# Ten segment banks in ten bursts in a row, and four rows of a unit by ScalarE's relu of a difference

## The chip, the cores and the metric

The kernel runs on one core of one Trainium2 chip. A core has five engines that run side by side: TensorE (matrix products), VectorE, ScalarE (activation functions), GpSimd and SyncE, which here only issues DMAs. TensorE writes to PSUM, eight banks of 128 partitions by 2 KB; VectorE and ScalarE read the banks. The metric is the device time of one execution in microseconds, the lower the better. In the profile PE is TensorE, PEld its weight loads, DVE is VectorE, ACT is ScalarE, POOL is GpSimd and SP is SyncE.

## The reference

Two attention layers over the same 2048 x 512 input are mixed by a sigmoid gate. Side A is full attention with 32 heads of 16 dimensions. Side B works in four segments of 512 rows: causal attention inside a segment, mixed with a linear memory of the earlier segments.

```python
def _A_ref(x, wqkv, wo):
    ...
    scores = jnp.einsum("bhqd,bhkd->bhqk", q, k) * scale
    p = _softmax(scores, axis=-1)
    o = jnp.einsum("bhqk,bhkd->bhqd", p, v)
    return (lambda x, *d: x.transpose(*d))(o, 0, 2, 1, 3).reshape(B, S, D) @ wo
...
    for s in range(N):
        qs, ks, vs = q[:, :, s], k[:, :, s], v[:, :, s]
        logits = jnp.einsum("bhqd,bhkd->bhqk", qs, ks) * scale + mask
        p = _softmax(logits, axis=-1)
        a_dot = jnp.einsum("bhqk,bhkd->bhqd", p, vs)
        ...
        o = g * a_mem + (1.0 - g) * a_dot
...
    a = _A_ref(x, A_wqkv, A_wo)
    b = _B_ref(x, B_wq, B_wk, B_wv, B_wo, B_beta)
    return g * a + (1 - g) * b
```

Every softmax needs the maximum of each row of scores. For side A a row has 2048 keys, in four chunks of 512.

## The kernel before

**Units and slots.** The work of both attentions is cut into units: four heads by 512 queries. A full-attention unit ("A", 32 of them) has 64 slots, a segment unit ("B", 32) has 10. They alternate A, B, A, B (line 102), so a pair has 74 slots, and all pairs have 2368. One slot of the main loop (line 1004) does two things with a bank of PSUM each:

- `score_part` (line 714): a product of 128 keys by 512 queries with the row maximum already subtracted (it stands in two extra rows of q), into one of three `st` banks; ScalarE takes the exp of it into `p` (line 752).
- `max_part` (line 214), for a slot 96 further on (`LEAD`): a product of 128 queries by 512 keys into one of four `sm` banks (`banks[m % 4]`), from which VectorE takes the maximum of each row. A unit needs all its maxima before its scores start; hence the lead.

The product of `score_part` uses one half of TensorE's rows and that of `max_part` the other, so the two of a slot run at once.

After each third slot (`BURST`) come value products (`some_values`, line 764; a handful of 128-query pieces, three or four as `most()` says, line 993), or three of the products of an output block or of a later q tile (`shared`, line 1017), and now and then the transpose of a unit's maxima (line 1027). What is issued between two such places is called a burst here: three score and three maximum products, and what follows them.

**Which bank is whose.** The list `maxs` (line 114) writes the order of the maximum products out by hand. A full-attention unit has 64 banks: four key chunks `kc`, four blocks `s` of 128 queries, four heads; one reduce over 512 columns each (line 226). A segment unit has ten banks with causal pieces: six with two pieces of 128 and 384 or of 256 and 256 columns, four with one piece of 512 (line 232). For these VectorE runs a fused add-and-minimum with a mask, and reads its accumulator out (line 238). The second piece of a bank is issued only after the next bank's reduce (`flush_rows`). A segment unit's banks stand among those of a full-attention unit, always at the first slot of a burst, at distances of 9 and 3 slots in turn (`apart`, line 119): two bursts with one, two without. In the first and last units they stand in each burst.

**Loads.** `load_q` and `load_k` (lines 147 and 157) bring a unit's q and a chunk of keys from DRAM by SyncE's queue, `PRE` = 20 slots ahead of their first maximum product. `NKA` = 8 and `NKB` = 2 buffers hold chunks of keys. A chunk goes in four DMAs: 32 and 16 rows for each half of TensorE's rows.

**Before the loop**, the first 310 us compute q, k and v of both sides (`qk_tile`, line 362, and `v_tiles`) and the memory, and the first 96 slots' maxima. Each q or k is split into two halves of the short fp32 type and stored in DRAM.

Of the kernel before, what the change touches and what calls it, by code (L numbers as in the profile page):

```python
# [19 lines left out]
D = 512  # L20
# [22 lines left out]
PRE = 20  # L43
NKA, NKB = 8, 2
# [3 lines left out]
def gated_mix(ctx, tc, x, xT, wqkv, a_wo, b_wq, b_wk, b_wv, b_wo, beta, gate_w, out):  # L48
# [96 lines left out]
    knext = {"A": 0, "B": 0}  # L145
# [11 lines left out]
    def load_k(u, kc):  # L157

        side, g, c = u
        t = kbuf[side][knext[side] % len(kbuf[side])]  # L160
        knext[side] += 1
        src = kd[side, g // 2, kc]
        for r in range(2):
            hs = slice(4 * (g % 2) + 2 * r, 4 * (g % 2) + 2 * r + 2)
            nc.sync.dma_start(raw(t)[64 * r:64 * r + 32], src[:, hs])
            nc.sync.dma_start(raw(t)[64 * r + 32:64 * r + 48], src[0:16, hs])
        kt_[u, kc] = t
# [46 lines left out]
    def max_part(m, bank):  # L214
# [3 lines left out]
        if u not in pmt:  # L218
            pmt[u] = mp.tile([128, 4, 4] + [4] * (side == "A"), F32, tag="pm" + side, name="pm")
        pm = pmt[u]  # L220
        ps = bank()
        if side == "A":

            kc, s, h = i // 8, i % 8 // 2, 2 * r + i % 2
            max_product(ps, u, h, s, 0, CH, kt_[u, kc])
            nc.vector.tensor_reduce(pm[:, h, s, kc:kc + 1], ps, axis=AX.X, op=ALU.max)  # L226
            flush_rows()
# [35 lines left out]
    def loads(m):  # L263

        m = min(m, len(maxs) - 1)
        while loaded[0] <= m:
            u, (r, i) = maxs[loaded[0]]
            if loaded[0] == first_max[u]:
                load_q(u)
            kc = u[2] if u[0] == "B" else i // 8  # L270
            if (u, kc) not in kt_:
                load_k(u, kc)
            loaded[0] += 1
# [3 lines left out]
    with ExitStack() as p0:  # L277
# [84 lines left out]
        def qk_tile(side, w, xc, o, dst, then=None):  # L362

            ps = pr_ps.tile([128, CH], F32, tag="pr", name="pr")
# [6 lines left out]
            def e0():  # L371
                nc.scalar.copy(full, ps)  # L372
                nc.scalar.copy(q1, full)  # L373
                nc.sync.dma_start(dst[0:16].rearrange("d h t -> (d h) t"), raw(q1))
                if then:
# [100 lines left out]
        for c in range(NCH):  # L476
# [8 lines left out]
            for o in range(NO):  # L485
                qk_tile("A", wAk, xc, o, kd["A", o, c])
# [206 lines left out]

    tri["rest"] = dp.tile([128, CH], F32, name="rest")
# [309 lines left out]
    while n < nS or queue or beside or filled[0] < len(fill):  # L1004
# [5 lines left out]
        if m < nS:  # L1010
            loads(m + PRE)

            max_part(m, lambda: banks[m % 4])
        run_todo(m)
# [67 lines left out]
```

## Time and profile before

| what | value |
|---|---|
| time, median of 3 runs | 1786.52 us (1785.98 to 1787.45) |
| span of the profiled execution, first to last instruction | 1784.1 us |
| mean granted TensorE clock | 0.999 |
| TensorE busy, main loop (330 to 1700 us) | 1369.95 of 1370 us |
| VectorE busy, same stretch | 1367.91 us |
| ScalarE busy, same stretch | 1211.58 us |
| GpSimd busy, same stretch | 544.55 us |

No time of the profiled execution is known beside its span; the median of the runs is 2.4 us above it. In the views below a row reads: start and duration in us, engine, line of the kernel, operation, tile written <- tiles read, shapes, count; in brackets the idle time of the engine ahead of it and what ended it. Rows with a count over 1 are several instructions merged, from the first start to the last end. Instructions of an engine overlap in their fill, so a row of seven is shorter than seven times one. "x" in a view by stretches counts instructions.

### The profile page before, as it was taken

To read this page: it belongs to the slowest core of one execution; us is meant where nothing else is said; L and a number is where in the kernel's file an instruction comes from. 1 tells how busy PE (TensorE), PEld (TensorE's weight loads), DVE (VectorE), ACT (ScalarE), POOL (GpSimd) and SP (SyncE) were. 2 spreads that over 40 slices of the span, in tenths; PEclk is the share of its full clock that TensorE was granted. 3 is DMA by queue.
4 is the path that set the end of the run, shared out by engine and by line. 5 is a ranking of instruction groups with operands and counts; after the bars stand their busy time and mean duration, and the time that the engine had idled before them with its cause. 6 is when DMAs were issued, how large, how long until landed. Compare 5 with 4: busy or idle time off the path is not lost.

```text
span 1784.1 us, 40690 instructions
## 1 busy us (share of the span) xinstructions
PE 1774.3 (99%) x14945; PEld 913.3 (51%) x14945; DVE 1574.0 (88%) x3330; ACT 1437.8 (81%) x2753; POOL 641.0 (36%) x748
## 2 busy tenths in 40 slices
PE   9999999999999999999999999999999999999999
PEld 7887776444444444444444444444444444444444
DVE  4235777999999999999999999999999999999931
ACT  5455444888888888888888888888888888888884
POOL 3002222414161416443434343343434253435343
PEclk9999999999999999999999999999999999999999
DMA  6667556435463446645454545454545354544542
GB/s 222 211 222 258 190 192 191 140 97 146 107 165 108 134 121 174 152 132 135 132 139 128 146 127 145 128 145 113 154 111 154 118 141 116 147 121 136 144 162 61
DMA packets 142278, 261.55 MB, mean 147 GB/s; under 512 B 36312, under 2 KB 60408, under 8 KB 141568
## 3 DMA queue, kind: packets, MB, share of 16 engines
q1 hardware_dynamic: 140864, 257.82, 49.9%
q8 instruction: 119, 1.95, 0.5%
q0 software_dynamic: 1216, 1.14, 0.3%
q14 instruction: 79, 0.65, 0.1%
HBM read 174.39 MB, written 83.25 MB: 144 GB/s over the span
## 4 chain that ended last, share of the span: by engine, by line
PE 94%; DVE 2%; DMA 1%; ACT 1%; POOL 1%; issue 0%; SPq 0%; POOLq 0%; DVEq 0%; ACTq 0%
PE ops L786 33%; PE st L729 27%; PE sm L205 14%; PE pr L311 10%; PE ops L898 4%; PE ops L669 2%; PE sm L898 2%; POOL mn L377 1%; DMA raw<-xT 1%; PE num L499 0%; DVE pm L226 0%; DMA qdB<-q 0%; ACT ex L384 0%; DVE q L380 0%; PE mt_ps L196 0%
## 5 line engine op out<-in xcount | busy, mean ns | idle before, releaser
L752 ACT ACTIVATE p<-st 128x512 f32<-128x512 f32 x2261 | 1189.2, 600 | 152.8 <-PE sm L205 100.7
L226 DVE TENSOR_REDUCE pm<-sm 128x1 f32<-128x512 f32 x2048 | 1281.0, 683 | 11.8 <-PE sm L205 11.6
L729 PE MATMUL st<-qA,kA 50*128 50x512 f32 x2014 | 663.1, 432 | 0.0
L205 PE MATMUL sm<-kA,qA 48*128 48x512 f32 x2048 | 658.7, 428 | 0.2
L786 PE MATMUL ops<-p,vA 128*17 128x128 f32 (+3 forms) x6432 | 552.0, 441 | 0.0
L729 PEld LDWEIGHTS st<-qA,kA 50*128 50x128 f32 x2014 | 327.4, 185 | 415.2 <-ACT p L752 371.0
L205 PEld LDWEIGHTS sm<-kA,qA 48*128 48x128 f32 x2048 | 330.4, 185 | 15.6 <-issue 7.1
L848 POOL TENSOR_TENSOR rcp<-rec,minus 128x32 f32<-128x32 f32 x43 | 234.2, 5447 | 75.7 <-DMA rec<-dend 71.0
L238 DVE CUSTOM_DVE_ANT_0 rest<-sm,mask 128x128 f32<-128x128 f32 (+3 forms) x512 | 247.3, 483 | 1.9 <-PE sm L205 0.5
L786 PEld LDWEIGHTS ops<-p,vA 128*17 128x17 f32 x6432 | 130.4, 96 | 215.1 <-issue 190.1
L733 POOL TENSOR_SCALAR_AFFINE_SELECT p<-p 128x512 f32<-128x512 f32 x128 | 79.5, 637 | 324.1 <-ACT p L752 319.6
L205 PE MATMUL sm<-kB,qB 48*128 48x128 f32 (+3 forms) x512 | 166.0, 384 | 0.0
L729 PE MATMUL st<-qB,kB 50*128 50x512 f32 (+1 forms) x495 | 109.1, 329 | 0.3 <-ACT mt L199 0.3
L380 DVE TENSOR_TENSOR q<-full,q 128x512 fp32r<-128x512 f32 x56 | 38.9, 694 | 74.4 <-ACT q L373 74.4
L729 PEld LDWEIGHTS st<-qB,kB 50*128 50x128 f32 x495 | 69.8, 186 | 59.3 <-ACT p L752 48.8
L786 PE MATMUL ops<-p,vB 128*17 128x128 f32 (+3 forms) x1504 | 87.5, 350 | 0.0
L187 POOL CAST ms<-nm 128x16 fp32r<-128x16 f32 x32 | 6.7, 209 | 203.9 <-DVE nm L183 202.0
L205 PEld LDWEIGHTS sm<-kB,qB 48*128 48x128 f32 x512 | 79.9, 184 | 0.0
L377 POOL TENSOR_SCALAR mn<-full 128x512 f32<-128x512 f32 x24 | 35.7, 1489 | 101.7 <-ACT full L372 81.3
L372 ACT COPY full<-pr 128x512 f32<-128x512 f32 x56 | 32.7, 584 | 42.7 <-PE pr L311 42.4
L187 POOL CAST ms<-pm 128x16 fp32r<-128x16 f32 x32 | 6.3, 197 | 128.2 <-DVE pm L238 128.1
L864 POOL TENSOR_TENSOR v<-v,inv 128x512 f32<-128x512 f32 x31 | 39.9, 1286 | 25.7 <-DMA inv<-rdA 21.7
(188 smaller groups left out, 1628.9 us busy)
## 6 DMA issues: line engine op xcount, KB each, us to landing
kA<-kdA SPq DMA_DIRECT2D x256, 128.0 KB
vA<-vdA SPq DMA_DIRECT2D x31, 544.0 KB
kA<-kdA SPq DMA_DIRECT2D x256, 64.0 KB
kdA<-q SPq DMA_DIRECT2D x32, 256.0 KB
qdB<-q SPq DMA_DIRECT2D x32, 256.0 KB
qA<-qdA SPq DMA_DIRECT2D x64, 128.0 KB
kdB<-q SPq DMA_DIRECT2D x32, 256.0 KB
qB<-qdB SPq DMA_DIRECT2D x64, 128.0 KB
```

The costliest lines, as they stand in the source:

```text
L205: nc.tensor.matmul(ps[:, n0:n0 + n], rows(qt[u][:, :, s * 128:(s + 1) * 128], h, 48), rows(k[:, :, k0:k0 + n], h, 48), start=True, stop=True)
L226: nc.vector.tensor_reduce(pm[:, h, s, kc:kc + 1], ps, axis=AX.X, op=ALU.max)
L238: rows_left.append(lambda h=h, s=s, n0=n0, w=w: nc.vector.tensor_tensor_reduce(out=tri["rest"][:, 0:w], in0=ps[:, n0:n0 + w], in1=tri["mas ...
L311: nc.tensor.matmul(ps, l(a, k), r(b, k), start=(n == 0), stop=(n == 11))
L377: nc.gpsimd.tensor_scalar_min(ph["mn"], full, 0.0)
L729: nc.tensor.matmul(ps[:, n0:n0 + CH - q0], rows(k[:, :, b * 128:(b + 1) * 128], h, 50), rows(q[:, :, q0:], h, 50), start=True, stop=True)
L733: nc.gpsimd.affine_select(out=x, in_=x, pattern=[[0, 4], [1, 128]], base=0, channel_multiplier=-1, compare_op=ALU.is_ge, fill=0.0)
L752: nc.scalar.activation(p[:, h], ps, AF.Exp, scale=SCALE)
L786: nc.tensor.matmul(ops[32 * h:32 * h + 17, q0:q0 + 128 * w], v[:, 17 * h:17 * h + 17], p[:, h, c0:c0 + 128 * w], start=(i == 0), stop=done ...
L848: eng.tensor_tensor(r, rec, minus, op=ALU.pow)
L864: eng.tensor_mul(k["v"], k["v"], k["inv"])
L898: yield lambda i=i, x=x, w=w: nc.tensor.matmul(ps, t[:, b, x], halved[side][:, o, w], start=start and i == 0, stop=stop and i == 2)
```

## The change

Two things change in `maxs`, and the rest follows from them.

1. The ten banks of a segment unit stand at ten bursts in a row, from slot 42 of the 74 on, at distance 3. (First and last units stay as they were.)
2. In 29 of the 32 full-attention units (all but the first two and the last), the four rows with `s` = 0, one for each head, take their maximum over key chunks 3 and 4 (`kc` 2 and 3) together. The kernel stores the difference of chunk 3 and chunk 4 of k in DRAM (`dd`) before the loop. In place of the product with chunk 3 there is one with the difference ("D"), of which ScalarE takes the relu into SBUF. In place of the reduce of the product with chunk 4 ("E") VectorE adds the relu to the bank and takes the maximum in one instruction: max(a, b) = b + relu(a - b). The four D stand at the last slot of the third, fifth, sixth and eighth of the ten bursts (`OVER`), the E four to eleven slots later.

`PRE` falls from 20 to 17. There is one buffer for the difference chunk and there are two for the results of the relu. Each of these 29 units loads a difference chunk in four more DMAs.

```diff
-PRE = 20
-NKA, NKB = 8, 2
+PRE = 17
+NKA, NKB, NKD = 8, 2, 1
+PAIRED = (0,)
+OVER = (2, 4, 5, 7)
...
+    dd = [dr.tile([32, 8, CH], F32, name=f"dd{o}") for o in range(NO)]
...
+    def paired(u):
+
+        return u[0] == "A" and 1 < u[1] + NG * u[2] < NU - 1
+
     maxs = []
     for k in range(NU):
-        mine = {u: iter(range(32)) for u in range(2)}
+        both = paired(unit("A", k))
+        plain = {r: iter([(kc, s, h) for kc in range(NCH) for s in range(4) for h in range(2)
+                          if not both or kc < 2 or s not in PAIRED]) for r in range(2)}
+        wide_ = {r: iter([(s, h) for s in PAIRED for h in range(2)]) for r in range(2)}
+        placed = {}
         bs = [k - 1] if 0 < k < NU - 1 else [k - 1, k] if k else []
         theirs = {r: [(unit("B", b), (r, i)) for b in bs for i in range(5)] for r in range(2)}
-        start, apart = (33, (3, 3)) if k == 1 else (6, (9, 3)) if k < NU - 1 else (23, (3, 3))
+        start = 33 if k == 1 else 42 if k < NU - 1 else 23
         at_ = [next(m for m in range(len(maxs) + start, len(maxs) + start + 6) if m % 3 == 0)]
         while len(at_) < 10 * len(bs):
-            at_.append(at_[-1] + apart[len(at_) % 2])
+            at_.append(at_[-1] + 3)
+        over = [at_[j] + 2 for j in OVER] if both else []
         for m in range(len(maxs), len(maxs) + 64 + 10 * len(bs)):
             r = (m + 1) % 2
             if m in at_ and bs:
                 maxs.append(theirs[r].pop(0))
-            else:
-                maxs.append((unit("A", k), (r, next(mine[r]))))
-        assert not theirs[0] and not theirs[1]
+                continue
+            i = placed.pop(m, None)
+            if m in over:
+                assert i is None
+                sh = next(wide_[r])
+                i = ("D", *sh)
+                placed[next(e for e in range(m + 4, m + 12, 2) if e not in at_ and e not in over and e not in placed)] = ("E", *sh)
+            maxs.append((unit("A", k), (r, i or next(plain[r]))))
...
-            kc, s, h = i // 8, i % 8 // 2, 2 * r + i % 2
-            max_product(ps, u, h, s, 0, CH, kt_[u, kc])
-            nc.vector.tensor_reduce(pm[:, h, s, kc:kc + 1], ps, axis=AX.X, op=ALU.max)
-            flush_rows()
+            kc, s, h = i[0], i[1], 2 * r + i[2]
+            max_product(ps, u, h, s, 0, CH, kt_[u, 3 if kc == "E" else kc])
+            if kc == "D":
+                excess[u, h, s] = ex = tri["pool"].tile([128, CH], F32, tag="over", name="over")
+                nc.scalar.activation(ex, ps, AF.Relu)
+            elif kc == "E":
+
+                nc.vector.tensor_tensor_reduce(out=tri["rest"], in0=ps, in1=excess.pop((u, h, s)), scale=1.0, scalar=-3.0e38,
+                                               op0=ALU.add, op1=ALU.max, accum_out=pm[:, h, s, 3:4])
+                flush_rows()
+            else:
+                nc.vector.tensor_reduce(pm[:, h, s, kc:kc + 1], ps, axis=AX.X, op=ALU.max)
+                flush_rows()
...
+        def apart_tile(o, ps):
+
+            t = wk1.tile([128, CH], F32, tag="ex", name="apart")
+            d = [wk.tile([128, CH], F32R, tag="ph", name="apart", bufs=4) for _ in range(2)]
+            nc.vector.tensor_sub(t, kept.pop(o), ps)
+            nc.gpsimd.tensor_copy(d[0], t)
+            nc.gpsimd.tensor_sub(d[1], t, d[0].bitcast(F32))
+            for i in range(2):
+                post(2, i, lambda i=i: nc.sync.dma_start(dd[o][16 * i:16 * i + 16].rearrange("d h t -> (d h) t"), raw(d[i])))
...
+    tri["pool"] = ctx.enter_context(tc.tile_pool(name="ov", bufs=2, reuse_waits="tile"))
+    kbuf["D"] = [dp.tile([128, 2, CH], F32R, name=f"kD{i}") for i in range(NKD)]
```

`qk_tile` calls `apart_tile` for the k tiles of chunk 4, and leaves those of chunk 3 in a bank (`kept`) until then. `load_k` takes its source from `dd` for a difference chunk. The maxima of full-attention units stand in two fixed tiles (`pmA`) whose place for chunk 3 of the paired rows is filled once with a very low number.

More of the change, by code (lines that the diff above doesn't have):

```diff
@@ L126, in gated_mix @@
                 maxs.append(theirs[r].pop(0))
-            else:
-                maxs.append((unit("A", k), (r, next(mine[r]))))
-        assert not theirs[0] and not theirs[1]
+                continue
[6 more added lines that the diff above has]
+            maxs.append((unit("A", k), (r, i or next(plain[r]))))
+        assert not theirs[0] and not theirs[1] and not placed
+        assert not any(next(i, None) for i in (*plain.values(), *(wide_.values() if both else ())))
     last_max = {u: m for m, (u, _) in enumerate(maxs)}
@@ L217, in max_part @@
         side, g, c = u
-        if u not in pmt:
-            pmt[u] = mp.tile([128, 4, 4] + [4] * (side == "A"), F32, tag="pm" + side, name="pm")
+        if u not in pmt and side == "A":
+            k = g + NG * c
+            pmt[u] = pmA[k % 2]
+            if k in (2, 3):
+                for s in PAIRED:
+                    nc.vector.memset(pmt[u][:, :, s, 2], -3.0e38)
+        elif u not in pmt:
+            pmt[u] = mp.tile([128, 4, 4], F32, tag="pmB", name="pm")
         pm = pmt[u]
@@ L1013, in gated_mix @@
             max_part(m, lambda: banks[m % 4])
+            used[0] = n
         run_todo(m)
```

26 lines of the change are left out of this document (20 added, 6 removed).

## The prediction

> **What bounds the kernel now.** I read the engine shares first, then busy time by stretch, then the order of time inside two bursts.
>
> ```profile
> span 1784.1 us, 40690 instructions
> PE 1774.3 (99%) x14945; PEld 913.3 (51%) x14945; DVE 1574.0 (88%) x3330; ACT 1437.8 (81%) x2753; POOL 641.0 (36%) x748
> ...
> core 0: us, PE busy (x) PEld busy (x) DVE busy (x) ACT busy (x) POOL busy (x), PEclk, DMA share, GB/s
> 330.00:1700.00 1370.00, 1369.95 (x12818) 631.54 (x12816) 1367.91 (x2934) 1211.58 (x2346) 544.55 (x630) 1.00 0.48 133
> 1033.20:1169.90 136.70, 136.70 (x1281) 62.95 (x1280) 136.50 (x292) 120.88 (x235) 57.16 (x64) 1.00 0.48 134
> 1677.20:1705.40 28.20, 28.20 (x263) 12.01 (x261) 28.20 (x79) 24.33 (x49) 17.99 (x17) 1.00 0.60 165
> 0.00:310.00 310.00, 304.70 (x1382) 230.08 (x1383) 169.60 (x309) 152.75 (x263) 59.98 (x79) 0.99 0.64 212
> ```
>
> From 330 to 1700 us both TensorE and VectorE are busy all the time, at full clock; ScalarE is at 88%. The second stretch is three pairs of units, 45.57 us a pair, or 1.847 us for each of its 24.67 bursts of three slots. Two engines at 100% do not say which one waits, so I look inside.
>
> ```profile
> 1060.13 4.26 DVE L226 TENSOR_REDUCE pm<-sm 128x1 f32<-128x512 f32 x7
> ...
> 1060.62 0.49 PE L729 MATMUL st<-qA,kA 50*128 50x512 f32 x1
> ...
> 1060.97 0.39 PE L729 MATMUL st<-qA,kA 50*128 50x512 f32 x1
> ...
> 1061.16 1.57 ACT L752 ACTIVATE p<-st 128x512 f32<-128x512 f32 x3 [0.32 <-PE sm L205]
> 1061.20 0.39 PE L205 MATMUL sm<-kA,qA 48*128 48x512 f32 x1
> ...
> 1061.53 1.06 PE L786 MATMUL ops<-p,vA 128*17 128x384 f32 x16
> ...
> 1062.52 0.50 PE L729 MATMUL st<-qA,kA 50*128 50x512 f32 x1
> ...
> 1062.86 0.62 PE L729 MATMUL st<-qA,kA 50*128 50x512 f32 x2
> ...
> 1063.05 1.57 ACT L752 ACTIVATE p<-st 128x512 f32<-128x512 f32 x3 [0.32 <-PE sm L205]
> ...
> 1063.42 0.84 PE L786 MATMUL ops<-p,vA 128*17 128x384 f32 x8
> ...
> 1064.19 0.50 PE L729 MATMUL st<-qA,kA 50*128 50x512 f32 x1
> ```
>
> Each burst is three score/maximum pairs (0.34 us to the second, 0.23 to the third, 0.33 to the values) and then value products. With four value pieces it lasts 1.90 us (1060.62 to 1062.52), with three 1.67 (to 1064.19). VectorE's seven reduces take 4.26 us; with 0.683 for the last (its mean, below), the other six step by 0.597, so three take 1.79. ScalarE's three exps take 1.57; less 0.60 for the last, they step by 0.485, and then ScalarE idles 0.32. So TensorE issues without a gap here and sets the beat; VectorE is 2% behind it, ScalarE has room.
>
> ```profile
> 901.32 0.96 PE L898 MATMUL ops<-wA,blk 128*128 128x512 f32 x3
> ...
> 903.15 0.96 PE L898 MATMUL ops<-wB,blk 128*128 128x512 f32 x3
> ```
>
> A pair has 74 value pieces and, in four further bursts, twelve output products; such a burst takes 1.83 us. TensorE's own need of a pair is then 20.67 bursts x (1.67 + 0.58 x 0.23) = 37.3, plus 4 x 1.83 = 7.3, plus about 0.25 for the transposes of maxima: 44.8 us. Against 45.57, 0.73 us of a pair is waiting and extras. Over the 29 units that change this is 21 us: **the ceiling of any gain**.
>
> Where those 0.73 us are:
>
> ```profile
> 1070.71 0.29 DVE L238 CUSTOM_DVE_ANT_0 rest<-sm,mask 128x128 f32<-128x128 f32 x1
> ...
> 1070.98 0.69 DVE L226 TENSOR_REDUCE pm<-sm 128x1 f32<-128x512 f32 x1
> ...
> 1071.59 0.55 DVE L238 CUSTOM_DVE_ANT_0 rest<-sm,mask 128x384 f32<-128x384 f32 x1
> ...
> 1071.85 0.50 PE L729 MATMUL st<-qA,kA 50*128 50x512 f32 x1
> ...
> 1072.06 1.88 DVE L226 TENSOR_REDUCE pm<-sm 128x1 f32<-128x512 f32 x3
> ...
> 1072.53 0.40 PE L729 MATMUL st<-qA,kA 50*128 50x512 f32 x1
> 1072.86 0.84 PE L786 MATMUL ops<-p,vA 128*17 128x128 f32 x16
> 1073.64 0.49 PE L729 MATMUL st<-qA,kA 50*128 50x512 f32 x1
> ...
> 985.59 0.42 DVE L238 CUSTOM_DVE_ANT_0 rest<-sm,mask 128x256 f32<-128x256 f32 x1
> 985.93 0.69 DVE L226 TENSOR_REDUCE pm<-sm 128x1 f32<-128x512 f32 x1
> ...
> 986.28 0.49 PE L729 MATMUL st<-qB,kB 50*128 50x512 f32 x1
> ...
> 986.62 0.39 PE L729 MATMUL st<-qB,kB 50*128 50x512 f32 x1
> 987.01 0.19 PEld L205 LDWEIGHTS sm<-kA,qA 48*128 48x128 f32 x2 [0.32 <-DVE pm L238]
> ```
>
> A segment bank with two pieces is held long: first piece (0.27 us for 128 columns, 0.34 for 256), the reduce of the next bank (0.60), second piece (0.47 or 0.34). Until then the product four slots on, the second of the next burst, cannot use the bank. The burst at 1071.85 has three value pieces yet takes 1.79 us: 0.12 lost. At 987.01 the product comes 0.39 us behind its partner. These are the waits that a lighter VectorE removes.
>
> **The change part by part.**
>
> ```profile
> L226 DVE TENSOR_REDUCE pm<-sm 128x1 f32<-128x512 f32 x2048 | 1281.0, 683 | 11.8 <-PE sm L205 11.6
> L238 DVE CUSTOM_DVE_ANT_0 rest<-sm,mask 128x512 f32<-128x512 f32 x128 | 87.6, 684 | 0.0
> L380 DVE TENSOR_TENSOR q<-full,q 128x512 fp32r<-128x512 f32 x56 | 38.9, 694 | 74.4 <-ACT q L373 74.4
> ```
>
> *VectorE.* In each of 29 units four pairs of reduces become four fused add-and-maximum instructions. The 512-column form (684 ns) costs what a reduce costs (683), so a pair loses 4 x 0.60 = 2.4 us of VectorE, 69 us in all. Per pair VectorE has 64 x 0.597 + 4 x (0.27 + 0.47 + 0.34 + 0.60) = 44.9, as much as TensorE's 44.8; it falls to 42.5.
>
> *TensorE.* The number of products is the same: one with the difference chunk and one with chunk 4 for one each with chunks 3 and 4. Cost 0.
>
> *Ten bursts in a row.* VectorE's need per burst is 2.0 us for the first two (0.27 + 0.47 or 0.68, and two reduces at 0.60: 1.88 to 1.94), 1.28 in the third, 1.88, 1.34, 1.34, 1.80, 1.20, 1.80, 1.80 after it; TensorE's mean is 44.8 / 24.67 = 1.81. The stretch 1677.20 to 1705.40 is fifteen segment bursts in a row already in this kernel, without relus: 1.88 us each, 0.03 over the mean. So a bare row of ten would cost 0.3 us a pair, the relus from the third burst on take that away, and the first two or three leave about 0.15 a pair. The run now falls on slots whose score products all belong to a full-attention unit, so it no longer meets the segment unit's split score products, as it does at 986.28.
>
> *Waits taken away.* One pair shows 0.12 (1071.85); the place at 986.28 costs 0.3 to 0.4, not in every pair. Bounds per pair 0.12 and 0.73; I take 0.5, nearer the ceiling since the waits recur at each second two-piece bank.
>
> *ScalarE.* 116 relus of 128x512 from a bank, nearest row the exp: 0.485 a step; bounds 0.485 and 0.60 (no overlap). A burst with a relu needs 4 x 0.485 = 1.94: 0.04 over a long burst, 0.27 over a short one. What waits behind it is the next burst's exps, then the score banks. The slack there comes from the rows: exps ending 1062.73 against the third score product at 1063.10 (0.37), and 1064.62 against about 1064.77 (0.15). A single relu is hidden by ScalarE's idle 0.32. The two in neighbouring bursts (fifth and sixth) pile up 0.08 to 0.54, so 0 to 0.4 a pair comes through; I take 0.1, since at 3.58 value pieces a burst more than half are long.
>
> The Trainium skill ("ScalarE: Activation LUTs", section "Rules for kernel authors") speaks against this: it wants relu on VectorE rather than ScalarE, VectorE being up to about 3 times as fast in bf16. The f32 rows here show no such ratio, 0.597 a step against 0.485; by the rule's ratio a relu would cost an estimated 1.8 us, and rival B would hold.
>
> *Loads.* Four more issues a pair on SP's queue for the difference chunk, and loads come 17 slots ahead in place of 20: 10.5 us for 12.3 (0.616 a slot).
>
> ```profile
> 1061.49 0.38 SPq L165 DMA_DIRECT2D kA<-kdA  x1
> 1061.91 0.42 SPq L166 DMA_DIRECT2D kA<-kdA  x1
> ```
>
> An issue takes about 0.4 us, so 1.6 of SP's 45 us. Chunk 4 is loaded earlier in a unit, the segment keys later; I take 0, and 0.2 a pair if a load were late.
>
> *Before the loop.* Four VectorE subtractions (0.69 us), eight GpSimd operations and eight 256 KB stores. TensorE is at 304.7 of 310 there, VectorE at 169.6: hidden, 0 to 2.8 us, I take 0.5.
>
> **The sum.** Per pair -0.5 + 0.15 + 0.1 = -0.25, x 29 = -7.3; plus 0.5: 1784.1 - 6.8 = 1777.3 as a span. The runs' median is 2.4 us above that span, so about **1779.5 us**. With the edges 0.73 and nothing lost: -21, 1765; with 0.12 won and 0.15 + 0.4 lost: +12.5, 1799.
>
> **The rivals.**
>
> *A, nothing to see:* the new row of bursts makes as many waits as it ends (0.3 a pair, as at 1677.20), because VectorE comes into it with a backlog. Time 1783 to 1790. For it: VectorE's 2% distance. Against it: fourteen plain bursts ahead of the row need 1.79 of 1.81 us each.
>
> *B, slower:* the relus sit in ScalarE's in-order queue and hold back exps. It decides if a relu steps by over 0.75 us, or waits for VectorE to free one of the two buffers of relu results: then a relu burst needs 2.2 us against 1.81, four of them 1.5 a pair, some 0.9 after recovery in the bursts between, less 0.35 won: +16 us, **1802**. For it: slack of only 0.15 in short bursts. Against it: 0.32 us idle a burst.
>
> *C, VectorE alone is the bound:* then the 69 us come out whole, 1718; half of it 1752. For it: 1367.91 of 1370 busy. Against it: the gapless order on TensorE.
>
> *D, table loads:*
>
> ```profile
> L569 ACT ACT_TABLE_LOAD x1 | 1.3, 1283 | 0.0
> ```
>
> Were relu to need another table than exp, 232 loads of 1.28 us would add 298 us: 2084. The order of the changed kernel's instructions has the same five loads as before, none near the relus. The skill (same page, "Table sets: the hidden batching unit") lists relu in exp's own set; no run so far shows it.
>
> **How the numbers follow.** Forecast (1771 to 1783) 0.52; A 0.20; B 0.20; C 0.07; D 0.01. A measurement of this kernel tells about 0.2%, 3.6 us, from no change. Faster by more: forecast and C, 0.59; within: A, 0.20; slower: B and D, 0.21. The forecast's own range is 1771 to 1783; to leave out no more than 2 in 10, the range reaches through A into B and a little into C: 1767 to 1798.
>
> **What would show it.** Right: VectorE's busy share in the loop falls by about 5% (2.4 of 44.9 us a pair), TensorE stays at 100%, short bursts after two-piece banks take 1.67 rather than 1.79, and a pair is 45.2 to 45.4 us. The relu's mean is about 600 ns and exps wait behind it only in the sixth and seventh burst of the row. Wrong: bursts with a relu over 2.0 us (B); the row's first three bursts at 1.9 or more with waits on VectorE (A); a pair under 44.5 us, which my TensorE count excludes (C). Products waiting on loads would show the shorter lead.

## The result, and the profile after

The kernel became slower: 1801.05 us (median of 4 runs, 1798.46 to 1803.20) against 1786.26 us before on the same chip (4 runs, 1785.98 to 1787.45), a ratio of 1.0083 (95% interval 1.0069 to 1.0097). The prediction said 1779.5 us, with a range of 1767 to 1798. The profiled execution took 1798.46 us, 1.8 more than its span.

The head of the page of the changed kernel, three rows of its view by stretches (the middle one holds the same three pairs of units as the second row in the prediction), and the groups that the change touches (busy us, mean ns of one | idle time before them):

```profile
span 1796.7 us, 41298 instructions
PE 1782.8 (99%) x14945; PEld 915.0 (51%) x14945; DVE 1521.7 (85%) x3336; ACT 1480.6 (82%) x2869; POOL 650.6 (36%) x756
```

```profile
core 0: us, PE busy (x) PEld busy (x) DVE busy (x) ACT busy (x) POOL busy (x), PEclk, DMA share, GB/s
330.00:1700.00 1370.00, 1369.12 (x12760) 630.34 (x12754) 1305.28 (x2908) 1248.35 (x2449) 535.66 (x617) 1.00 0.52 141
...
1043.04:1180.31 137.27, 137.27 (x1283) 63.00 (x1282) 130.83 (x292) 125.39 (x246) 57.29 (x64) 1.00 0.52 143
...
0.00:310.00 310.00, 301.10 (x1361) 227.59 (x1362) 170.29 (x311) 149.11 (x258) 66.86 (x83) 0.99 0.65 215
```

```profile
L264 DVE CUSTOM_DVE_ANT_0 rest<-sm,over 128x512 f32<-128x512 f32 x116 | 79.5, 686 | 9.2 <-ACT p L813 3.5
...
L261 ACT ACTIVATE over<-sm 128x512 f32<-128x512 f32 x116 | 71.9, 620 | 0.0
```

VectorE did get lighter: busy for 95% of the three pairs (130.83 of 137.27) where it was 99.9%. TensorE is still busy all the time, and yet the three pairs take 0.57 us longer. The instruction that adds and takes the maximum takes 686 ns and relu 620, as the prediction had them. None of these totals shows a loss. Before the loop TensorE has 3.6 us less work behind it at 310 us (301.10 against 304.70): the loop starts late.

To find the rest I took the start of each burst (its first maximum product) in both traces and compared the same slots. The first maximum product comes 4.7 us later than before; from the first to the last the loop is 8.2 us longer, as these rows show (the group of the maximum products, first and last start):

```profile
L205 PE MATMUL sm<-kA,qA x2048: 386/397/506, 170.2 to 1707.4; 48*128 48x512 f32 x187
```

```profile
L232 PE MATMUL sm<-kA,qA x1932: 386/398/511, 174.9 to 1720.4; 48*128 48x512 f32 x194
```

The loop's difference is a sum of both signs. Bursts that became shorter gained 14.2 us in all, 0.49 a pair; 12.3 us of it are in bursts that held or followed a two-piece bank in the old order. The others lost 22.4: the seventh of the row 0.22 us in every one of the 29 units (6.3 us), its first, second, fifth and sixth, which hold two-piece banks, 0.04 to 0.09 each in the mean, its tenth 0.07, and a handful of bursts 0.3 to 1.2 us at once.

The seventh burst, seen from VectorE and from TensorE in one unit of the changed kernel (start, duration, engine, line, operation):

```profile
1063.88 0.29 DVE L280 CUSTOM_DVE_ANT_0 rest<-sm,mask 128x128 f32<-128x128 f32 x1 [0.47 <-PE sm L232]
1064.10 0.08 DVE L280 DVE_READ_ACCUMULATOR2_ANT pm<- 128x1 f32 x1
1064.33 0.69 DVE L264 CUSTOM_DVE_ANT_0 rest<-sm,over 128x512 f32<-128x512 f32 x1
1064.94 0.08 DVE L264 DVE_READ_ACCUMULATOR2_ANT pmA<- 128x1 f32 x1
1065.06 0.56 DVE L280 CUSTOM_DVE_ANT_0 rest<-sm,mask 128x384 f32<-128x384 f32 x1
```

```profile
1065.24 0.50 PE L790 MATMUL st<-qA,kA 50*128 50x512 f32 x1
1065.24 0.50 PE L232 MATMUL sm<-kB,qB 48*128 48x512 f32 x1
1065.58 0.40 PE L790 MATMUL st<-qA,kA 50*128 50x512 f32 x1
1065.68 0.53 PE L232 MATMUL sm<-kA,qA 48*128 48x512 f32 x2
1066.02 0.40 PE L790 MATMUL st<-qA,kA 50*128 50x512 f32 x1
1066.35 0.84 PE L847 MATMUL ops<-p,vA 128*17 128x128 f32 x16
1067.12 0.50 PE L790 MATMUL st<-qA,kA 50*128 50x512 f32 x1
```

The sixth burst holds a two-piece bank and, right behind its first piece, an add (line 264). The add starts 0.45 us after the piece of 128 columns, and the second piece 0.73 after the add. Over the whole trace the median steps are 444 and 734 ns. A plain reduce in the same place (`f1_plain`, below) follows the piece after 266 and gives way after 608. The bank is therefore free only at 1065.62. The maximum product that needs it, the second of the next burst, starts at 1065.68, a tenth behind its score product (1065.58). From there the two products of a slot no longer start together, and the burst, with three value pieces, lasts 1.88 us (1065.24 to 1067.12) in place of 1.67.

### The profile page after: what moved, and what is told of

It reads as the page before. It is cut to its first block, busy times and chain, and to the rows that moved or that the text cites. A ratio compares the mean times of both kernels' runs of the same rounds, so it can differ in the third digit from the quotient of the medians.

```text
span 1796.7 us, 41298 instructions
## 1 busy us (share of the span) xinstructions
PE 1782.8 (99%) x14945; PEld 915.0 (51%) x14945; DVE 1521.7 (85%) x3336; ACT 1480.6 (82%) x2869; POOL 650.6 (36%) x756
## 4 chain that ended last, share of the span: by engine, by line
PE 93%; DMA 2%; DVE 1%; ACT 1%; POOL 1%; issue 1%; SPq 0%; POOLq 0%; DVEq 0%; ACTq 0%
PE ops L847 33%; PE st L790 27%; PE sm L232 14%; PE pr L353 9%; PE ops L959 4%; PE ops L728 2%; PE sm L959 2%; POOL mn L436 1%; DMA raw<-xT 1%; PE kept L353 1%; PE num L558 1%; DMA qdB<-q 0%; PE mt_ps L223 0%; ACT ex L443 0%; PE mps L589 0%
## 5 line engine op out<-in xcount | busy, mean ns | idle before, releaser
L268 DVE TENSOR_REDUCE pmA<-sm 128x1 f32<-128x512 f32 x1816 | 1131.6, 680 | 17.0 <-PE sm L232 15.3
L790 PE MATMUL st<-qA,kA 50*128 50x512 f32 x2014 | 671.0, 433 | 0.0
L232 PE MATMUL sm<-kA,qA 48*128 48x512 f32 x1932 | 634.7, 431 | 1.0 <-DVE pmA L268 0.7
L232 PEld LDWEIGHTS sm<-kA,qA 48*128 48x128 f32 x1932 | 312.4, 184 | 18.1 <-issue 7.2
L264 DVE CUSTOM_DVE_ANT_0 rest<-sm,over 128x512 f32<-128x512 f32 x116 | 79.5, 686 | 9.2 <-ACT p L813 3.5
L261 ACT ACTIVATE over<-sm 128x512 f32<-128x512 f32 x116 | 71.9, 620 | 0.0
```

Source lines behind the costliest of these rows:

```text
L232: nc.tensor.matmul(ps[:, n0:n0 + n], rows(qt[u][:, :, s * 128:(s + 1) * 128], h, 48), rows(k[:, :, k0:k0 + n], h, 48), start=True, stop=True)
L261: nc.scalar.activation(ex, ps, AF.Relu)
L264: nc.vector.tensor_tensor_reduce(out=tri["rest"], in0=ps, in1=excess.pop((u, h, s)), scale=1.0, scalar=-3.0e38, op0=ALU.add, op1=ALU.max, ...
L790: nc.tensor.matmul(ps[:, n0:n0 + CH - q0], rows(k[:, :, b * 128:(b + 1) * 128], h, 50), rows(q[:, :, q0:], h, 50), start=True, stop=True)
```

## The experiments

All times are medians, beside 1785.6 to 1786.7 us of the kernel before on the same chips.

**The row alone, and the lead.** `e4_ten_only` keeps the row of ten bursts and the lead of 17, without differences, relus and adds; `e1_pre20` is the changed kernel with the old lead; `e7_ten_pre20` is the bare row with the old lead.

```diff
-PAIRED = (0,)
+PAIRED = ()
```

```diff
-PRE = 17
+PRE = 20
```

> Ten segment banks in ten bursts in a row and the lead of 17, but no relu, no difference chunk and nothing of it before the loop. Theory: the 4.3 us before the loop are gone, the 0.22 us of each row's seventh burst too; the waits after the old places are gone and new ones on VectorE stand in the row: 1786 to 1791. Rival (the bare row runs at VectorE's 1.88 us a burst as the last unit's row does, 0.3 us a pair): 1795 to 1797.

> The changed kernel with loads 20 slots ahead again, all else as changed. Theory (late loads): some ten single stalls of 0.2 to 1.2 us, in which a maximum product waits long after VectorE is done with its bank while SyncE has only just issued the key chunk, come from the lead of 17 slots. Then they go: 1796 to 1797, and the spread of the runs (1798.5 to 1803.2) narrows. Rival (the four more DMAs of a pair and their place alone make them late, the lead does not matter): 1800 to 1801.

> Only the row of ten bursts, without relu and without difference chunk, with the lead of 20 slots that the kernel before has. Theory: the bare row at a lead of 17 (1785.07) still has two key loads that come late for 1.4 and 0.7 us; with 20 they vanish: 1781 to 1784. Rival, the lead only moves which buffer is waited for: 1785 to 1787.

Measured: `e4_ten_only` 1785.07 (ratio 0.9993, 0.9984 to 1.0003), `e1_pre20` 1797.69 (1.0062, 1.0047 to 1.0077), `e7_ten_pre20` 1783.72 (0.9985, 0.9975 to 0.9994). So the bare row is no slower than the old order, and with the old lead it is a little faster than both kernels. The bare row came out below its expected 1786. The lead of 17 costs 3.4 us in the changed kernel and 1.4 in the bare row. One place where it costs, in the changed kernel:

```profile
701.35 0.30 SPq L192 DMA_DIRECT2D kA<-kdA  x1
701.70 1.11 SPq L193 DMA_DIRECT2D kA<-kdA  x1
...
706.00 0.69 DVE L268 TENSOR_REDUCE pmA<-sm 128x1 f32<-128x512 f32 x1
...
706.80 0.18 PEld L232 LDWEIGHTS sm<-kA,qA 48*128 48x128 f32 x1 [1.11 <-DVE pmA L268]
...
706.83 0.69 PE L232 MATMUL sm<-kA,qA 48*128 48x512 f32 x2 [0.71 <-DVE pmA L268]
```

The row blames a VectorE reduce, but that reduce frees another bank. The two pieces of keys that this product reads were issued at 701.35 and 701.70, and their semaphores are complete only at 706.42 and 706.69: the keys are late. This burst loses 1.2 us with the lead of 17, and in `e1_pre20` it loses nothing.

**ScalarE's part.** `e5_relu32` runs relu over 32 of the 512 columns (the maxima of the paired rows leave out what chunk 3 has above chunk 4 in the others; the two buffers are zeroed once ahead of the loop).

```diff
-                nc.scalar.activation(ex, ps, AF.Relu)
+                nc.scalar.activation(ex[:, 0:32], ps[:, 0:32], AF.Relu)
```

> The changed kernel with a relu over 32 of the 512 columns only (the other 480 add 0, so the maximum leaves out part of chunk 3). ScalarE's part of each relu falls by about 0.4 us, all waits stay. Theory 1 (the 0.22 us of the seventh burst come from VectorE, which holds the segment bank of the sixth burst until the fused instruction and the second piece are done): no change, 1799 to 1802. Rival (two relus in neighbouring bursts hold back the exps on ScalarE): the seventh burst takes 1.67 and 1.88 again and the time falls by 6 us, 1794 to 1796.

Measured: 1798.39 (1.0067, 1.0052 to 1.0082), 2.7 us less, between the two expected ranges. The seventh burst still loses 0.22 us. What goes is the loss of the tenth burst, 0.067 us in the mean, which falls to nothing. Relu costs something, but it is not the main loss.

**Where the relus and adds stand.** `e3_over2367` and `e6_over0257` move them to other bursts of the row; `e6_over0257` also keeps an add from directly following the first slot of the first six bursts.

```diff
-OVER = (2, 4, 5, 7)
+OVER = (2, 3, 6, 7)
```

```diff
-OVER = (2, 4, 5, 7)
+OVER = (0, 2, 5, 7)
...
-... for e in range(m + 4, m + 12, 2) if e not in at_ and ...
+... for e in range(m + 4, m + 14, 2) if e not in at_ and e - 1 not in at_[:6] and ...
```

> The changed kernel with the four relus in the third, fourth, seventh and eighth burst of the row: two pairs of neighbouring relus, and no fused instruction between the two pieces of a segment bank. Theory 1 (VectorE's hold): the 0.22 us are gone, 6 us less, 1794 to 1796. Rival (neighbouring relus on ScalarE): there are two such places, 6 us more, 1806 to 1808.

> The four relu bursts of a row stand first, third, sixth and eighth in place of third, fifth, sixth and eighth, and the instruction that adds and takes the maximum is never served by VectorE directly before or behind a segment bank in two pieces of the same burst. Theory held: a fused VectorE instruction directly behind another fused one comes 0.13 to 0.26 us late (443 against 205 ns from the short piece to the add, 738 against 472 between two pieces), the bank in two pieces is held that long, and the seventh burst of the row then loses 0.22 us in each of 29 units: 6.4 us go, 1794 to 1796. Rival 1, the number of relus and adds itself sets the loss wherever they stand: 1800 to 1802. Rival 2, any relu in the first burst meets ScalarE with exps due and moves the loss there: the first burst loses 0.2 or more, 1800 to 1808.

Measured: `e3_over2367` 1809.38 (1.0130, 1.0113 to 1.0147) and `e6_over0257` 1831.50 (1.0252, 1.0232 to 1.0271). In the first, the seventh burst loses 0.39 and the eighth 0.23 in the mean, 17.9 us in all. That is near the rival's figure, two places with neighbouring relus on ScalarE, but by luck: `h3_place2367` below takes this loss away with the relus where they are. The second expectation missed by 36 us, for two reasons. First, I had the neighbours wrong: the second piece of a bank is issued behind the next reduce, so an add at the third slot of a two-piece burst stands between a piece and the next bank's piece. This is such a place in `e6_over0257`, where the seventh burst loses 0.4 us in every unit and the second about 0.3 in most (20.3 us in all):

```profile
898.86 0.69 DVE L264 CUSTOM_DVE_ANT_0 rest<-sm,over 128x512 f32<-128x512 f32 x1
899.48 0.08 DVE L264 DVE_READ_ACCUMULATOR2_ANT pmA<- 128x1 f32 x1
899.71 0.29 DVE L280 CUSTOM_DVE_ANT_0 rest<-sm,mask 128x128 f32<-128x128 f32 x1
...
900.53 0.55 DVE L280 CUSTOM_DVE_ANT_0 rest<-sm,mask 128x384 f32<-128x384 f32 x1
```

From the add to the next piece it is 0.85 us, and the two-piece bank comes free at 901.08; the maximum product that needs it starts at 901.14, 0.26 behind its score product. Second, the difference chunk, needed in the first burst of the row there, came late in some units: the first bursts lose 17 us in all, one of them took 5.8 us, and the trace puts 6.4 us of TensorE's waits down to that chunk's DMAs. Both together cost far more than the 6.4 us that were to be won.

`e8_all` has the order of `e6_over0257`, the lead of 20 and the stores of the difference chunk one slot later.

```diff
-                post(2, i, lambda i=i: nc.sync.dma_start(dd[o]...
+                post(1, 2 + i, lambda i=i: nc.sync.dma_start(dd[o]...
```

> The order 0, 2, 5, 7 of the relu bursts, the lead of 20 slots again, and the stores of the difference chunk posted one slot after the subtraction rather than two to three. If the three losses (6.4 us in the seventh burst, 3.4 us of late key loads, 4.3 us before the loop) are separate and each is taken away by its own edit: 1801.05 - 6.4 - 3.4 - 2 to 4 = 1787 to 1789. If they share a cause or one gives back what another takes: above 1793. If the stores of the difference chunk are not what delays the stretch before the loop, that stretch keeps its 4.3 us and the time is 1790 to 1792.

Measured: 1819.88 (1.0189, 1.0174 to 1.0204), over 30 us above what was expected, spoiled by the same order; only its start is of use, below. (With `post(2, i)` the store is put two slots on, with `post(1, 2 + i)` one slot on, in its second half.)

**The add beside a plain reduce.** `f1_plain` makes the add a plain reduce in the same place, `f2_sep` puts a memset of one column ahead of and behind each add.

```diff
-                nc.vector.tensor_tensor_reduce(out=tri["rest"], in0=ps, in1=excess.pop((u, h, s)), ...
+                excess.pop((u, h, s))
+                nc.vector.tensor_reduce(pm[:, h, s, 3:4], ps, axis=AX.X, op=ALU.max)
```

```diff
+                nc.vector.memset(tri["sep"], 0.0)
                 nc.vector.tensor_tensor_reduce(out=tri["rest"], ...
+                nc.vector.memset(tri["sep"], 0.0)
```

> The changed kernel with one thing undone: the instruction that adds relu's result and takes the maximum is a plain maximum reduce of the bank (so the maxima leave out what chunk 3 has above chunk 4; the difference product and its relu run as before, and the relu's result is not read). VectorE has as many instructions in the same places, of the same 512 columns. Theory held, a fused instruction directly behind a fused one starts 0.13 to 0.26 us late: the step from a segment piece of 128 columns to this instruction falls from 443 to 205 ns, from this instruction to a segment piece from 733 to 605, the seventh burst of the row loses its 0.22 us, the ones before and after it with an add some 0.03: 6 to 8 us less, 1793 to 1795.5. Rival, the loss belongs to the difference product and the relu in their bursts (ScalarE frees that bank, not VectorE): 1800 to 1802.

> The changed kernel with a VectorE memset of one column directly before and directly behind each of the 116 adds, so that no fused instruction stands directly behind a fused one. If only the direct neighbour pays (something of the two overlaps badly), the step from a piece of 128 columns to the add is some 205 + 125 = 330 ns in place of 443, and the seventh burst's loss falls from 0.22 to under 0.1 us: 1796 to 1799. If the second fused instruction has to wait until the first one's accumulator is read, whatever stands between, and the memset comes on top: the same 443 or more, 1801 to 1804.

Measured: `f1_plain` 1794.08 (1.0042, 1.0026 to 1.0058), `f2_sep` 1799.35 (1.0071, 1.0055 to 1.0087). The same bursts as above in `f1_plain`:

```profile
1062.74 0.29 DVE L280 CUSTOM_DVE_ANT_0 rest<-sm,mask 128x128 f32<-128x128 f32 x1 [0.47 <-PE sm L232]
...
1063.01 0.69 DVE L265 TENSOR_REDUCE pmA<-sm 128x1 f32<-128x512 f32 x1
1063.62 0.55 DVE L280 CUSTOM_DVE_ANT_0 rest<-sm,mask 128x384 f32<-128x384 f32 x1
```

The second piece starts 0.88 us after the first (1062.74 to 1063.62) where it was 1.18 (1063.88 to 1065.06), and the seventh burst's loss falls from 0.216 to 0.003 us in the mean of 29 (rows of TensorE's, from its first product to that of the burst behind it: 1.68 us):

```profile
1064.09 0.50 PE L790 MATMUL st<-qA,kA 50*128 50x512 f32 x1
...
1065.77 0.49 PE L790 MATMUL st<-qA,kA 50*128 50x512 f32 x1
```

So 7.0 us are the add beside its neighbours. In `f2_sep`, whose time lies between the two expected ranges, the seventh burst still loses 0.216:

```profile
1066.38 0.29 DVE L282 CUSTOM_DVE_ANT_0 rest<-sm,mask 128x128 f32<-128x128 f32 x1 [0.46 <-PE sm L232]
...
1066.63 0.06 DVE L264 MEMSET sep<- 128x1 f32 x1
1066.83 0.69 DVE L265 CUSTOM_DVE_ANT_0 rest<-sm,over 128x512 f32<-128x512 f32 x1
```

The memset starts 0.25 us after the piece, and the add still comes 0.45 us after it. It is the add that is waiting, whatever stands between.

**What it waits for.** The piece and the add both write their elementwise result, which nobody reads, into one scratch tile, `rest`. In the compiled order of VectorE's instructions (the accumulator reads between them left out) each of them carries a wait for VectorE itself:

```
L280 ISA rest,pm<-sm_3045,mask 128x128 [waits DVE_49,PE_49]
L264 ISA rest,pmA_207<-sm_3046,over 128x512 [waits DVE_49,PE_49]
L280 ISA rest,pm<-sm_3045,mask 128x384 [waits DVE_49]
```

The semaphore waited for is the one that the accumulator read behind the last writer of `rest` raises. All 116 adds carry this wait in the changed kernel, and none does in `h1_place`.

`h1_place` lets the add write over the relu's result; `h2_place_fix` is the same with the lead of 20 and the later stores; `h3_place2367` the same in the order of `e3_over2367`.

```diff
-                nc.vector.tensor_tensor_reduce(out=tri["rest"], in0=ps, in1=excess.pop((u, h, s)), ...
+                ex = excess.pop((u, h, s))
+                nc.vector.tensor_tensor_reduce(out=ex, in0=ps, in1=ex, ...
```

> The changed kernel with one word changed: the add-and-maximum writes its elementwise result, which nobody reads, over the relu's result and no longer into the scratch tile that the segment pieces write too. It then carries no wait for VectorE's own earlier instructions. Theory 1, the 0.13 to 0.26 us behind a fused instruction are a wait for the last writer of the shared scratch tile: the step from a segment piece of 128 columns to the add falls from 443 to 205 ns and from the add to a piece from 733 to 605, the seventh burst's 0.22 us go, and the time is that of the plain reduce: 1793 to 1795.5. Theory 2, the accumulator has to be read before the next fused instruction starts: nothing changes, 1800 to 1802.

> The same, with the lead of 20 slots and the stores of the difference chunk one slot later (1795.34 with the shared scratch tile). Theory 1: 1787.5 to 1789.5, that is 1785.8 of the kernel with all four causes away plus ScalarE's relu (2.7). Theory 2: 1794.5 to 1796.

> The relu bursts third, fourth, seventh and eighth (1809.38 with the shared scratch tile, 18.6 us of it in the seventh and eighth bursts), with the add writing over the relu's result. Theory 1: those bursts lose nearly nothing, 1790 to 1796. Theory 2: 1808 to 1811.

Measured: `h1_place` 1792.58 (1.0039, 1.0026 to 1.0053; its six runs lie between 1787.9 and 1797.0), `h2_place_fix` 1787.46 (1.0010, 1.0001 to 1.0019), `h3_place2367` 1797.86 (1.0082, 1.0061 to 1.0103). The first two are within half a us of their expected ranges. The third lost its 17.9 us in the seventh and eighth bursts (0.1 us is left), yet it is 2 us above its range: its ninth burst now loses 0.12 and its tenth 0.09 us in the mean, 6.3 us in all, with score products that wait for exps behind the two neighbouring relus. So this price on ScalarE exists too, once VectorE is out of the way:

```profile
1069.46 0.18 PEld L791 LDWEIGHTS st<-qA,kA 50*128 50x128 f32 x1 [0.30 <-ACT p L814]
```

The same bursts as above in `h1_place`:

```profile
1061.90 0.29 DVE L281 CUSTOM_DVE_ANT_0 rest<-sm,mask 128x128 f32<-128x128 f32 x1 [0.46 <-PE sm L232]
1062.11 0.08 DVE L281 DVE_READ_ACCUMULATOR2_ANT pm<- 128x1 f32 x1
1062.16 0.69 DVE L265 CUSTOM_DVE_ANT_0 over<-sm,over 128x512 f32<-128x512 f32 x1
1062.78 0.08 DVE L265 DVE_READ_ACCUMULATOR2_ANT pmA<- 128x1 f32 x1
1062.78 0.55 DVE L281 CUSTOM_DVE_ANT_0 rest<-sm,mask 128x384 f32<-128x384 f32 x1
```

Median steps: from the piece to the add 267 ns (444 with the shared tile, 266 for the plain reduce in the same place), from the add to the second piece 616 (734 and 608). The accumulator is read as before, and the next fused instruction starts beside the read. So the wait for the last writer of the shared tile was the cause, and the accumulator itself does not hold the next instruction back. An add that carries no such wait steps like a plain reduce in its place.

**Before the loop.** `b1_dd_only` is the kernel before with the difference chunk computed and stored, and nothing that reads it; `f4_nostore` is the same without the eight stores; `g2_pre20_late` is the changed kernel with the lead of 20 and the stores one slot later (the edit shown for `e8_all`).

> The kernel before with the four subtractions, the eight GpSimd operations and the eight stores of the difference chunk ahead of the loop, and nothing that reads it; loop, bursts and lead as before. Theory: these operations delay the stretch before the loop by 4.3 us and the loop not at all: 1789.5 to 1791.5, and the first maximum product starts about 4.3 us later than in the kernel before. Rival, that stretch hides them and the 4.3 us come from the loads and products that stand in another order at the loop's start: 1785.5 to 1787.5.

> The kernel before with the four subtractions and eight GpSimd operations of the difference chunk ahead of the loop, without the eight stores (nothing reads the chunk). With the stores it took 1792.1 against 1786.7. Theory: GpSimd waits for the stores to free its two tiles, and VectorE, ScalarE and the weight loads queue behind: 1786.5 to 1788 without them. Rival, the subtractions, or the banks and GpSimd steps themselves, delay the stretch: 1790 to 1792.

> The change as it is meant, with the lead of 20 slots and the stores of the difference chunk one slot later. Only the lead: 1797.7. If the later stores give back the 3.5 us by which the first maximum product came earlier where they were posted so (172.7 against 176.3): 1793.5 to 1795. If that stretch is late for another reason: 1797 to 1798.5.

Measured: `b1_dd_only` 1792.12 (1.0029, 1.0018 to 1.0040), `f4_nostore` 1786.20 (1.0002, 0.9992 to 1.0011), `g2_pre20_late` 1795.34 (1.0052, 1.0037 to 1.0067), 2.35 us less than `e1_pre20`. The stores alone make the 5.5 us of `b1_dd_only`. In the view of waits from 90 to 180 us (total us, times, longest), the changed kernel first, `f4_nostore` below:

```profile
POOL apart L409 <- DMA dd<-apart: 10.5, 2, 6.6
...
DVE apart L408 <- POOL apart L410: 8.2, 3, 4.4
...
ACT wqh L389 <- DMA raw<-b_wq: 5.8, 2, 3.2
```

```profile
DVE apart L367 <- POOL apart L369: 5.0, 3, 1.9
...
ACT wqh L348 <- DMA raw<-b_wq: 3.2, 2, 2.3
```

GpSimd waits for a store to free its tile, VectorE's subtraction waits for GpSimd, and the splitting of the next input tiles and weights (line 390) stands behind that subtraction in VectorE's queue. SyncE's queue, in the changed kernel, closes the ring:

```profile
111.33 6.93 SPq L380 DMA_DIRECT2D raw<-b_wq  x2
118.35 0.42 SPq L412 DMA_DIRECT2D dd<-apart  x1
```

```profile
115.96 0.69 DVE L408 TENSOR_TENSOR apart<-kept,full 128x512 f32<-128x512 f32 x1 [4.43 <-POOL apart L410]
...
117.16 1.89 DVE L390 TENSOR_TENSOR xl<-raw,xh 128x512 fp32r<-128x512 f32 x3
```

The two issues of a weight load hold that queue for 6.93 us, and the stores that GpSimd needs are behind them. The second is issued at 117.88, when the first of VectorE's three splits behind the late subtraction is done (117.85) and its buffer is free. TensorE, as the same stretch of three kernels shows (before, changed, `f4_nostore`), then lacks 3 us of work:

```profile
90.00:180.00 90.00, 89.29 (x411) 71.17 (x410) 42.79 (x77) 49.18 (x85) 12.97 (x12) 1.00 0.72 239
```

```profile
90.00:180.00 90.00, 86.08 (x392) 67.82 (x390) 41.10 (x75) 46.19 (x81) 20.54 (x19) 1.00 0.75 248
```

```profile
90.00:180.00 90.00, 89.40 (x411) 71.32 (x409) 46.25 (x80) 48.76 (x85) 22.82 (x20) 1.00 0.75 240
```

With the stores one slot later the first maximum product comes at 173.0 us in `e8_all` and 174.4 in `g2_pre20_late`, against 176.6 in `e1_pre20` and 170.6 in `e7_ten_pre20`, which has no difference chunk. This start varies: in the profiles of the ten kernels that have the eight stores in their first place it lies between 174.5 and 177.4.

**Relus and adds away from the row.** `f3_front` puts them ahead of the row, with chunks 1 and 2 in place of 3 and 4, the lead of 20 and the later stores.

```diff
-OVER = (2, 4, 5, 7)
+OVER = (-8, -7, -5, -4)
...
-        over = [at_[j] + 2 for j in OVER] if both else []
+        over = [at_[0] + 3 * j + 2 for j in OVER] if both else []
...
-            if c == 2:
+            if c == 0:
...
-                if c == 3:
+                if c == 1:
```

> The four differences and adds of a unit stand in bursts ahead of the row of ten (eighth, seventh, fifth and fourth burst before it; chunks 1 and 2 in place of 3 and 4, so that the keys are there), the row is bare, the lead is 20, and the stores of the difference chunk are posted one slot later. Theory: no add stands next to a segment bank, so nothing is lost in the row (that of the bare row of ten at a lead of 20: 1783.7); before the loop 2.5 to 6 us are lost (first maximum product 172.7 to 176.3 against 170.2); VectorE, 2.4 us lighter a pair just ahead of the row, gives back the 0.16 us of the burst before it and more (4.7 us): 1781 to 1786. Rival 1, the relus and adds cost some 0.2 us a pair wherever they are: 1790 to 1794. Rival 2, late loads of the difference chunk, as where its first product stood in the row's first burst: over 1800.

Measured: 1806.95 (1.0113, 1.0095 to 1.0131). That is rival 2's range, but not its cause. The row itself, now without adds, is as that of `e7_ten_pre20`, burst by burst. But the first product comes 8 us later (the difference is now made earlier; that this is why was not tested), and the loop loses 18 us ahead of the row, by the starts of the same slots. The most, 8.7 us, is lost in the sixth burst before the row, which takes up to 2.42 us where it took 1.85. ScalarE's rows there, with the row of TensorE's loads that waits for it:

```profile
1280.95 0.67 ACT L261 ACTIVATE over<-sm 128x512 f32<-128x512 f32 x1
1281.43 0.67 ACT L851 COPY oraw<-ops 128x512 f32<-128x512 f32 x1
```

```profile
1282.15 0.53 PEld L959 LDWEIGHTS ops<-wA,blk 128*128 128x128 f32 x3 [0.67 <-ACT oraw L851]
```

A relu in front of the copy of a finished value bank holds up the output products behind that copy. This is the prediction's rival B, ScalarE's queue, at a place where a copy is due; in the changed kernel's row an exp follows each of the 116 relus.

**All causes at once.** `g1_all_undone` is the changed kernel with the lead of 20, the later stores, the plain reduce of `f1_plain` and the short relu of `e5_relu32`.

> The changed kernel with all four suspected causes taken away at once: lead of 20 slots, the stores of the difference chunk one slot later, the add a plain maximum reduce (the maxima leave out what chunk 3 has above chunk 4), and relu over 32 of 512 columns. The difference products, their loads and their places stay. If the four causes are all there is, the time is that of the bare row of ten at a lead of 20 (1783.7) plus some 2.5 us that the later stores still cost before the loop, less what VectorE's lighter row may give (nothing to 4.7): 1782 to 1787. If they overlap, or something else of the difference product costs (its loads, its weights): above 1789.

Measured: 1785.79 (0.9998, 0.9988 to 1.0008). Taken away one at a time the four are 7.0 + 3.4 + 2.7 + 2.35 = 15.4 us, which would give 1785.6. They add up. What is left against the bare row (1783.72) is 2.1 us, and the start is still 3.5 us late (174.1 for 170.6), so the later stores gave back only a part of that cost; nothing else of the change costs time that these runs can tell.

## Why the prediction was wrong

- *TensorE cost 0, relu some 600 ns, no table loads:* held. Relu measured 620 ns and stepped by 0.48 us, and there are five table loads as before. The Trainium skill ("ScalarE: Activation LUTs", section "Table sets: the hidden batching unit") puts relu in exp's own set, and the trace agrees.
- *Waits taken away, 0.5 a pair:* held in size, 0.49 (14.2 us over 29 pairs), but not for the reason given, "the waits that a lighter VectorE removes". The bare row `e7_ten_pre20`, where VectorE is as loaded as before, gains 14.0. The new place of the banks removes them.
- *Ten bursts in a row, +0.15 a pair:* too small. First to last maximum product is 1534.2 us in `e7_ten_pre20` against 1537.2 before (170.2 to 1707.4), a net gain of 0.10 a pair; with 0.48 won, 0.38 are given back, some 0.3 of it in the row and the burst ahead of it. That is the prediction's 0.3 for a bare row. The relus were to take half of it away and did not: the row's first six bursts lose as much with them (0.26 a pair) as without (0.23). The 21 us called the ceiling were mostly not to be had by a new order.
- *ScalarE's relus, +0.1 a pair:* held, 2.7 us or 0.09 a pair. They cost it in the tenth burst, not in the sixth and seventh.
- *VectorE 2.4 us a pair lighter, "the 512-column form (684 ns) costs what a reduce costs (683)":* **this step failed.** VectorE's busy time fell by 1.9 us a pair (136.50 to 130.83 over three), and the duration is right. The steps are not. A duration does not contain the wait ahead of an instruction. In the kernel before, a plain reduce always stood between two fused instructions, so their shared scratch tile never made one wait. The change puts the add beside the pieces: 444 ns for 266 and 734 for 608, in a bank that the next burst needs. That was 7 to 8.5 us (`f1_plain`, `h1_place`), a term missing from the sum. VectorE's spare time did not help, since the loss is the lateness of one bank, not the engine's load.
- *Loads 0, bounds to 0.2 a pair:* mis-sized, 3.4 us or 0.12 a pair, within the bounds.
- *Before the loop 0.5 us, 0 to 2.8:* **failed.** The bound counted the work of the added operations beside an idle VectorE. What counted was the order: a store late on SyncE's queue, GpSimd waiting for it, VectorE's queue behind GpSimd. 4.7 us in the changed kernel's profile, 5.5 in `b1_dd_only`.
- *The rivals:* B named 1802 us, close to the 1801.05, but that is luck, for its reason did not occur: no relu waited for its buffer (its group has 0.0 us of idle time ahead of it) and none stepped by 0.75 us (0.55 at most). A's price for a bare row, 1783 to 1790, is what `e4_ten_only` and `e7_ten_pre20` took. C and D fell.

Term by term, the sum of -6.8 us comes out as -3.0 for the row, +2.7 for relu, +7.0 for the adds' waits, +3.4 for the lead and +4.7 before the loop: +14.8, and the medians differ by 14.8. The terms are from different pairs of runs, medians and single profiles, each good to 1 us or worse, so that they close to a tenth is luck. (The prediction's sum has a slip: 1777.3 and 2.4 are 1779.7, not 1779.5.)

The repaired change (`h2_place_fix`) is at 1787.46, no gain over the kernel before; the best of all is the bare row with the old lead, 1783.72, 0.15% below it (0.06 to 0.25%). What remains of the repaired change's loss is relu on ScalarE and a start that is 2.7 us late (the first maximum product at 173.3 us against 170.6 in `e7_ten_pre20`). Lighter work on VectorE bought nothing that shows: `g1_all_undone`'s loop is 0.5 us shorter than that of `e7_ten_pre20` (1533.7 against 1534.2).

## What to carry to other kernels

A new instruction is priced by its duration and by what it must wait for in its new place; look for every tile that it writes, also those whose content nobody reads, and give each kind of instruction its own. Where banks rotate as here, look at the instruction that frees a bank: a lighter engine was no help when that one instruction came later. A store that frees a tile has a place in a queue like any work: before a step is called hidden, follow which queue its release goes through.

## What the runs showed of the hardware

A VectorE instruction that waits for VectorE's own previous write starts 0.23 us (1064.10 to 1064.33) or 0.12 us (1064.94 to 1065.06) after the accumulator read in front of it begins. Without that wait it is 0.05 us (1062.11 to 1062.16) and nothing (1062.78). So a wait for one's own engine costs time, although the add comes behind the piece in any case. A memset of one column slips in between (1066.63 in `f2_sep`) and does not shorten the wait. And a burst in which the products of a slot start 0.1 us apart, not together, lasted 0.2 us longer (1.88 against 1.68 us for the same pieces, 1064.09 to 1065.77 in `f1_plain`); why 0.1 us grows to 0.2 no run here shows.
